# Storing the intermediate x2 once as float32, by feature block from three buffers, and splitting it in the second layer pair

## The chip, the cores and the metric

The kernel runs on one core of a Trainium2 chip. The metric is device microseconds of one execution, the median of several runs. Besides the timed runs there is one execution under the hardware profiler; all rows below are from it.

Five engines work side by side, each through its own list in order: TensorE (PE, its weight loads shown as PEld), VectorE (DVE), ScalarE (ACT), GpSimd (POOL) and SyncE (SP), which here only issues DMAs. Engines wait for each other through semaphores.

## The reference

```python
# attention with a forgetting gate, 4 x 8 heads, 768 steps, head size 48
for t in range(S):
    state = f[:, :, t, :, None] * state + einsum('bhd,bhe->bhde', k[:, :, t], v[:, :, t])
    y[:, :, t] = einsum('bhd,bhde->bhe', q[:, :, t], state)
x = y.transpose(0, 2, 1, 3).reshape(3072, 384)
# first pair of layers: 384 -> 2048 -> 384
h = x @ w_in
x2 = where(h > 0, h, exp(minimum(h, 0)) - 1) @ w_out
# second pair: 384 -> 1024 -> 384
out = ((x2 @ w1) * (x2 @ w2) @ w3) @ w_out2
```

All arrays are float32. The weights arrive as float64 bit patterns and are turned into float32 on the core.

## The kernel before

Matrix products of the two layer pairs run on operands that were split into two parts: hi, a rounded copy in the matmul format (fp32r), and lo, the float32 value minus hi. One float32 product is then three matmuls: hi by hi, hi by lo, lo by hi. The split of a tile is an ACT copy that rounds (hi) and a DVE subtract (lo).

**First pair.** The 3072 tokens are 8 tiles of 384 (index j). A tile is 16 units (index m, one unit per 128 of the 2048 hidden features); the running unit number is U. Unit U does, in this order: some attention work for the next tile; `p1_in(U)`, 9 matmuls into a PSUM bank `h` (line 584), ACT and DVE make `g` from it (587, 588, 590); `p1_split(U-1)`, which splits g (602, 603); `p1_out(U-2)`, 9 matmuls into the three PSUM banks `acc0` to `acc2`, one per block of 128 output features (616). So a tile's sums are complete two units into the next tile. Each of the three acc banks exists once, so the next tile's first matmul into a bank waits until the old sums have been read out of it.

**The end of a tile** is lines 618 to 625. For each of the three blocks i, ACT copies the bank to `oh`, DVE subtracts to get `ol`, and SP stores both to the scratch tensor `x2_scr` in HBM, which holds hi and lo of x2. The pool `o_p` has two buffers for `oh` and two for `ol`.

**Second pair.** The tokens are 6 tiles of 512, each of 8 units. `p2_load(j)` brings hi and lo of x2 for tile j from `x2_scr` in two DMAs, straight into the two matmul operands `xh` and `xl`. Unit U does `p2_in(U)`: 9 matmuls into `h`, 9 into `at` (810), an ACT copy of `h` to `a` (816), a DVE product with `at` (818) and a split of that (821, 822); and `p2_out(U-2)`: 9 matmuls into the acc banks (836). `h` has two banks. The load of tile 0 is called at unit 14 of the last first-pair tile, the load of tile j+1 in unit 2 of tile j.

**Order of the work.** Units 17 to 109 stand in the engines' lists in the order in which the code is written (`manual_schedule`). From unit 110 on, in the last two tiles of the first pair and in the whole second pair, a list scheduler of the framework sets the order on each engine. In that stretch there is much else to do: the weights of the second pair are loaded, turned into float32 by DVE (lines 81, 83, 86, 89, after an ACT step in line 74), split by ACT and POOL (509, 510), and w3 and w_out2 are multiplied together by PE in eight rows (671).

Of the kernel before, what the change touches and what calls it, by code (L numbers as in the profile page):

```python
# [9 lines left out]
F32 = mybir.dt.float32  # L10
F32R = mybir.dt.float32r
# [209 lines left out]
def main_path(ctx, tc, flag, qkf, vin, w_in, w_out, w1, w2, w3T, w_out2, ident_d, tri_d, x2_scr, out):  # L221
# [36 lines left out]
    def slot(part, k):  # L258
        return f"wb{k}" if part == "h" else "we" if k == 0 else f"wa{k - 1}"
# [346 lines left out]
    def p1_out(U):  # L606
        if not 0 <= U < NU:
            return
        j, m = divmod(U, MF)
        if m == 0:  # L610
            accs[j] = [acc_p.tile([128, 512], F32, name=f"acc{i}")[:, 0:TN] for i in range(KD)]
        ops = pairs(j, m, 1, gs.pop(U))
        for i in range(KD):
            c = slice(128 * i, 128 * i + 128)
            for n, (lw, rg) in enumerate(ops):
                nc.tensor.matmul(accs[j][i], lhsT=lw[:, 0, c], rhs=rg,  # L616
                                 start=(m == 0 and n == 0), stop=(m == MF - 1 and n == len(ops) - 1))
        if m == MF - 1:
            for i in range(KD):
                oh = o_p.tile([128, TN], F32R, name="oh")  # L620
                ol = o_p.tile([128, TN], F32R, name="ol")
                nc.scalar.activation(out=oh, in_=accs[j][i], func=AF.Copy)
                nc.vector.tensor_tensor(out=ol, in0=accs[j][i], in1=oh.bitcast(F32), op=ALU.subtract)  # L623
                for x, o in enumerate((oh, ol)):
                    nc.sync.dma_start(out=x2_scr[x, :, i, j * TN:(j + 1) * TN], in_=o.bitcast(F32))
            accs.pop(j)

    def start_late():
        att.close()
        late["u"] = ctx.enter_context(tc.tile_pool(name="u2", bufs=3))  # L630
        late["tmp"] = ctx.enter_context(ExitStack())
        late["o"] = late["tmp"].enter_context(tc.tile_pool(name="o2p", bufs=1))
        late["w3"] = late["tmp"].enter_context(tc.tile_pool(name="w3p", bufs=2))
        o2 = late["o2"] = [late["o"].tile([128, M2, DM], F32R, name=f"o2{x}") for x in "hl"]
        late["wf"] = {}
        late["row"] = 0
        late["w3t"] = {}
        late["base"] = len(jobs) + M2
        for k in range(M2):
            jobs.append((DM, [(whole(DM), wo2_u[128 * k:128 * k + 128, :])],  # L640
                         to_parts(o2[0][:, k, :], o2[1][:, k, :]), None))
        for i in range(M2):
            for k0 in (0, 4):
                src = w3T_u[128 * k0:128 * (k0 + 4), 256 * i:256 * (i + 1)].rearrange("(k p) n -> p k n", p=128)
                jobs.append((512, [(lambda f: f.rearrange("p (k n) -> p k n", k=4), src)], w3_part(i, k0), None))
        for _ in range(2):
            cv_load()
# [28 lines left out]
    xs = {}  # L676

    def p2_load(j):
        if j < NTILE2:
            xs[j] = [wp.tile([128, KD, TN2], F32R, name=slot(x, 5 + 2 * (j % 2))) for x in "hl"]  # L680
            for x, t in enumerate(xs[j]):
                nc.sync.dma_start(out=t.bitcast(F32), in_=x2_scr[x, :, :, j * TN2:(j + 1) * TN2])

    man = ExitStack()
    pro = ExitStack()
# [58 lines left out]
    for U in range(NU + LAG):  # L744
        j, m = divmod(U, MF)
        if U == MAN:
            man.enter_context(tc.manual_schedule())
        if U == MAN_B:
            man.close()
        if j == 0:  # L750
            while cv["main"] < at_job[0, m]:
                cv_step()
            quota[0] = T0_JOBS
        while lows and 2 * MF - len(lows) < 2 * (U - MF) + 4:
            low(*lows.pop(0))
        if j == 0:
            pass
        elif late:
            quota[0] = 1 + (late["row"] > rows_done)
        rows_done = late.get("row", 0)  # L760
        todo = at_slots[j > 0].get(m, []) if j < NTILE - 1 else []
        for early in (1, 0):
            for i, k in todo:
                if (k in EARLY) == early:
                    c = CPT * (j + 1) + i
                    steps[k](c)
                    if k == len(steps) - 1:
                        a_load(c + 2)
            if early and U < NU:
                p1_in(U, fill)  # L770
            if early and U >= 1:
                p1_split(U - 1)
        if j == 0 and m >= LAG:
            while cv["main"] < at_job[1, m - LAG]:
                cv_step()
        p1_out(U - LAG)
        while quota[0] > 0:
            fill()
        if j == NTILE - 2 and m == LATE_AT:
            start_late()  # L780
        if late:
            late["go"] = lambda i: U >= (NTILE - 1) * MF + 4 * (i // 4) + 3 + LAG
            w_rows()
            if j == NTILE - 1 and m % 4 == 3:
                for a in range(KD):
                    job_12(m // 4, a)
            if m == 14 and j == NTILE - 1:
                p2_load(0)
    while late["row"] < M2:
        cv_step(1)  # L790
        w_rows()
# [1 line left out]


    late["tmp"].close()
    N2 = NTILE2 * M2
    cs = {}

    def p2_in(U):
        j, m = divmod(U, M2)  # L800
        xh, xl = xs[j]
        wh, wl = w12[m // 2]
        c = slice(128 * (m % 2), 128 * (m % 2) + 128)
        ps = []
        for e in range(2):
            p = h_p.tile([128, 512], F32, name="h") if e == 0 else at_p.tile([128, 512], F32, name="at")
            n = 0
            for a in range(KD):
                for lw, rx in ((wh, xh), (wh, xl), (wl, xh)):
                    nc.tensor.matmul(p, lhsT=lw[:, a, e, c], rhs=rx[:, a, :],  # L810
                                     start=(n == 0), stop=(n == 3 * KD - 1))
                    n += 1
            ps.append(p)
            if e == 0:
                av = late["u"].tile([128, TN2], F32, name="a")
                nc.scalar.activation(out=av, in_=p, func=AF.Copy)  # L816
        cc = av
        nc.vector.tensor_tensor(out=cc, in0=ps[1], in1=av, op=ALU.mult)  # L818
        f = xt_p.tile([128, KD, TN], F32R, name="xh" if U % 2 else "xl").rearrange("p a t -> p (a t)")
        ch, cl = f[:, 0:TN2], f[:, TN2:2 * TN2]  # L820
        nc.scalar.activation(out=ch, in_=cc, func=AF.Copy)
        nc.vector.tensor_tensor(out=cl, in0=cc, in1=ch.bitcast(F32), op=ALU.subtract)
        cs[U] = (ch, cl)
# [24 lines left out]
    for U in range(N2 + LAG):  # L848
# [4 lines left out]
                cv_step()  # L853
        if U < N2:
            p2_in(U)
            if m == 2:
                p2_load(j + 1)
        while quota[0] > 0:
            fill()
        p2_out(U - LAG)  # L860
# [73 lines left out]
```

## Time and profile before

| | |
|---|---|
| runs | 884.84, 883.4, 884.22 us; median 884.22 |
| the profiled execution's own time | 883.1 us |
| its span, first to last instruction | 881.0 us |
| mean granted clock of TensorE | 0.993 of full speed |
| PE busy in the span | 845.7 us |
| DVE busy | 486.6 us |
| ACT busy | 400.1 us |
| first pair with attention | about 30 to 575 us |
| second pair | about 575 to 875 us |

The profiled execution is 1.1 us below the median and 0.3 below the lowest of the timed runs. A busy PE row counts a matmul from its start to its modelled end; since matmuls overlap, a new 128x384 one starts each 0.17 us while one alone is shown as 0.33.

### The profile page before, as it was taken

How to read it: one execution, taken by the hardware profiler on the slowest of the kernel's cores; microseconds unless marked ns; L12 is line 12 of the kernel's file. 1: busy time of each engine (PE TensorE's matmuls, PEld its weight loads, DVE VectorE, ACT ScalarE, POOL GpSimd, SP SyncE). 2: the span in 40 equal slices, each digit the busy share in tenths (PEclk: the TensorE clock that was granted, in tenths of full speed). 3: DMA queues.
4: the chain of work that ended last, by engine and by line, in shares of the span. 5: the costliest groups of instructions: out<-in, count | busy, mean ns of one | idle time of the engine just before them, and what ended most of it. 6: DMA issues, size and time to landing. Idle time of an engine off the chain costs nothing.

```text
span 881.0 us, 14419 instructions
## 1 busy us (share of the span) xinstructions
PE 845.7 (96%) x5767; PEld 741.5 (84%) x5767; DVE 486.6 (55%) x984; ACT 400.1 (45%) x785; POOL 74.9 (9%) x80
## 2 busy tenths in 40 slices
PE   7799999999999999999999899989999999999996
PEld 6465689999999999999899789968888888888885
DVE  7999687555455555464567997894222212222221
ACT  5766455455554564654655755643212212122211
POOL 3100000000000000000002323541000000000000
PEclk8999999999999999999999999999999999999999
DMA  9775131221311312213141644570202021030001
GB/s 268 217 221 168 42 96 44 62 78 43 97 43 44 96 43 53 87 43 85 55 133 41 211 145 142 192 225 21 88 20 72 36 68 41 1 107 1 36 1 39
DMA packets 43338, 77.16 MB, mean 88 GB/s; under 512 B 3376, under 2 KB 27184, under 8 KB 43264
## 3 DMA queue, kind: packets, MB, share of 16 engines
q1 hardware_dynamic: 43264, 76.17, 28.5%
q8 instruction: 47, 0.77, 0.4%
q14 instruction: 27, 0.22, 0.1%
HBM read 62.00 MB, written 14.16 MB: 86 GB/s over the span
## 4 chain that ended last, share of the span: by engine, by line
PE 77%; DVE 13%; DMA 4%; issue 3%; ACT 2%; POOL 1%; SPq 0%; DVEq 0%; POOLq 0%
PE acc L616 18%; PE h L584 17%; PE acc L836 11%; PE h L810 10%; PE at L810 10%; PE at L416 3%; PE at L355 2%; DVE wa L86 2%; DVE wa L89 2%; PE at L671 2%; DVE wa L81 2%; DMA x_scr<-ol 1%; DVE ol L623 1%; PE at L380 1%; PE at L361 1%
## 5 line engine op out<-in xcount | busy, mean ns | idle before, releaser
L616 PE MATMUL acc<-gh,wa 128*128 128x384 f32 x432 | 146.5, 370 | 0.0
L590 DVE SCALAR_TENSOR_TENSOR g<-r,h 128x384 f32<-128x384 f32 x112 | 61.7, 551 | 143.5 <-ACT r L588 143.5
L587 ACT ACTIVATE r<-h 128x384 f32<-128x384 f32 x128 | 62.4, 487 | 149.0 <-PE h L584 148.8
L818 DVE TENSOR_TENSOR a<-at,a 128x512 f32<-128x512 f32 x48 | 33.2, 691 | 172.0 <-PE at L810 170.8
L616 PE MATMUL acc<-gh,wb 128*128 128x384 f32 x336 | 116.9, 348 | 9.2 <-DVE ol L623 9.1
L584 PE MATMUL h<-xh,wa 128*128 128x384 f32 x348 | 118.3, 378 | 3.2 <-DVE gh L590 2.6
L584 PE MATMUL h<-xh,wb 128*128 128x384 f32 x336 | 113.6, 338 | 3.4 <-DVE g L590 3.4
L616 PE MATMUL acc<-gl,wb 128*128 128x384 f32 x336 | 112.5, 335 | 0.6 <-DVE gl L603 0.6
L584 PE MATMUL h<-xl,wb 128*128 128x384 f32 x336 | 112.3, 334 | 0.0
L616 PEld LDWEIGHTS acc<-gh,wa 128*128 128x128 f32 x432 | 80.7, 188 | 11.0 <-issue 0.2
L584 PEld LDWEIGHTS h<-xh,wa 128*128 128x128 f32 x348 | 65.1, 188 | 17.3 <-DVE gh L590 5.0
L816 ACT ACTIVATE a<-h 128x512 f32<-128x512 f32 x48 | 28.7, 597 | 110.7 <-PE h L810 110.7
L616 PEld LDWEIGHTS acc<-gh,wb 128*128 128x128 f32 x336 | 63.0, 188 | 13.9 <-DVE ol L623 12.1
L588 ACT ACTIVATE r<-r 128x384 f32<-128x384 f32 x128 | 67.1, 524 | 3.5
L584 PEld LDWEIGHTS h<-xh,wb 128*128 128x128 f32 x336 | 63.1, 188 | 5.1 <-DVE g L590 4.7
L616 PEld LDWEIGHTS acc<-gl,wb 128*128 128x128 f32 x336 | 63.1, 188 | 0.9 <-DVE gl L603 0.9
L584 PEld LDWEIGHTS h<-xl,wb 128*128 128x128 f32 x336 | 63.1, 188 | 0.4
L603 DVE TENSOR_TENSOR gl<-g,gh 128x384 fp32r<-128x384 f32 x112 | 62.9, 561 | 0.6 <-ACT gh L602 0.6
L602 ACT ACTIVATE gh<-g 128x384 fp32r<-128x384 f32 x112 | 57.3, 512 | 12.2 <-DVE g L590 12.1
L810 PE MATMUL h<-wb,wb 128*128 128x512 f32 x144 | 56.2, 390 | 3.1 <-ACT a L816 3.1
L810 PE MATMUL h<-wa,wb 128*128 128x512 f32 x144 | 56.0, 389 | 0.0
L810 PE MATMUL at<-wb,wb 128*128 128x512 f32 x144 | 56.0, 389 | 0.0
(145 smaller groups left out, 1537.9 us busy)
## 6 DMA issues: line engine op xcount, KB each, us to landing
qkf<-qkf_dram SPq DMA_DIRECT2D x21, 672.0 KB, 5.1
wst<-moe_w_out_dram SPq DMA_DIRECT2D x24, 384.0 KB, 3.7
wst<-moe_w_dram SPq DMA_DIRECT2D x16, 512.0 KB, 3.6
wst<-moe_w_in_dram SPq DMA_DIRECT2D x16, 384.0 KB, 4.2
wst<-moe_w_dram SPq DMA_DIRECT2D x24, 256.0 KB, 3.6
v<-vin_dram SPq DMA_DIRECT2D x23, 224.0 KB, 4.9
x_scr<-oh SPq DMA_DIRECT2D x24, 192.0 KB, 2.0
x_scr<-ol SPq DMA_DIRECT2D x24, 192.0 KB, 2.1
```

The source lines that it names most:

```text
L416: nc.tensor.matmul(yp[32 * i:32 * i + 32, a * CH:(a + 1) * CH], lhsT=w[:, i, w0:w0 + 32], rhs=x[:, i, :], start=(n == 0), stop=(n == len(o ...
L584: nc.tensor.matmul(hp, lhsT=lw, rhs=rx, start=(n == 0), stop=(n == len(ops) - 1))
L587: nc.scalar.activation(out=r, in_=hp, func=AF.Relu, scale=-1.0)
L588: nc.scalar.activation(out=r, in_=r, func=AF.Exp, scale=-1.0)
L590: nc.vector.scalar_tensor_tensor(out=g, in0=r, scalar=-1.0, op0=ALU.add, in1=hp, op1=ALU.max)
L602: nc.scalar.activation(out=gh, in_=g, func=AF.Copy)
L603: nc.vector.tensor_tensor(out=gl, in0=g, in1=gh.bitcast(F32), op=ALU.subtract)
L616: nc.tensor.matmul(accs[j][i], lhsT=lw[:, 0, c], rhs=rg, start=(m == 0 and n == 0), stop=(m == MF - 1 and n == len(ops) - 1))
L810: nc.tensor.matmul(p, lhsT=lw[:, a, e, c], rhs=rx[:, a, :], start=(n == 0), stop=(n == 3 * KD - 1))
L816: nc.scalar.activation(out=av, in_=p, func=AF.Copy)
L818: nc.vector.tensor_tensor(out=cc, in0=ps[1], in1=av, op=ALU.mult)
L836: nc.tensor.matmul(accs[j][i], lhsT=lw[:, m % 4, c], rhs=rc, start=(m == 0 and n == 0), stop=(m == M2 - 1 and n == 2))
```

## The change

The scratch tensor holds x2 once, as plain float32. At the end of a first-pair tile each of the three acc banks is copied out once: bank 0 and bank 2 by ACT, bank 1 by DVE, with no subtract. The blocks 0 and 1 go through the two buffers of `o_p`, block 2 through a buffer of its own (`gc`, from the attention pool, or from a new pool `g2` once the attention pools are closed). Three stores go out in place of six.

In the second pair a load brings three tiles of one feature block each (float32, 128x512). Tile 0 goes into the three buffers of pool `u2`, called at unit 10 of the last tile and split at unit 14; the others go into a new pool `f2` of six buffers, opened after the weight product is done, called in unit 1 of the tile before, and split one block per unit in units 3, 4 and 5. A split is, for each block, an ACT copy into `xh` (line 695 in the new file) and a DVE subtract into `xl` (696).

```diff
         if m == MF - 1:
             for i in range(KD):
-                oh = o_p.tile([128, TN], F32R, name="oh")
-                ol = o_p.tile([128, TN], F32R, name="ol")
-                nc.scalar.activation(out=oh, in_=accs[j][i], func=AF.Copy)
-                nc.vector.tensor_tensor(out=ol, in0=accs[j][i], in1=oh.bitcast(F32), op=ALU.subtract)
-                for x, o in enumerate((oh, ol)):
-                    nc.sync.dma_start(out=x2_scr[x, :, i, j * TN:(j + 1) * TN], in_=o.bitcast(F32))
+                o = late["g"].tile([128, TN], F32, name="gc") if i == 2 and late else (
+                    e_p.tile([128, TN], F32, name="gc") if i == 2 else o_p.tile([128, TN], F32, name="o"))
+                if i % 2:
+                    nc.vector.tensor_copy(out=o, in_=accs[j][i])
+                else:
+                    nc.scalar.activation(out=o, in_=accs[j][i], func=AF.Copy)
+                nc.sync.dma_start(out=x2_scr[:, i, j * TN:(j + 1) * TN], in_=o)
             accs.pop(j)
...
+        late["g"] = ctx.enter_context(tc.tile_pool(name="g2", bufs=1))
...
     def p2_load(j):
         if j < NTILE2:
-            xs[j] = [wp.tile([128, KD, TN2], F32R, name=slot(x, 5 + 2 * (j % 2))) for x in "hl"]
-            for x, t in enumerate(xs[j]):
-                nc.sync.dma_start(out=t.bitcast(F32), in_=x2_scr[x, :, :, j * TN2:(j + 1) * TN2])
+            pool, nm = (late["u"], "a") if j == 0 else (late["f"], "f")
+            xs[j] = [pool.tile([128, TN2], F32, name=nm) for a in range(KD)]
+            for a, f in enumerate(xs[j]):
+                nc.sync.dma_start(out=f, in_=x2_scr[:, a, j * TN2:(j + 1) * TN2])
+
+    def p2_split(j, blocks=range(KD)):
+        if j < NTILE2:
+            if 0 in blocks:
+                xp[j] = [wp.tile([128, KD, TN2], F32R, name=slot(x, 5 + 2 * (j % 2))) for x in "hl"]
+            xh, xl = xp[j]
+            for a in blocks:
+                f = xs[j][a]
+                nc.scalar.activation(out=xh[:, a], in_=f, func=AF.Copy)
+                nc.vector.tensor_tensor(out=xl[:, a], in0=f, in1=xh[:, a].bitcast(F32), op=ALU.subtract)
...
+            if m == 10 and j == NTILE - 1:
+                p2_load(0)
             if m == 14 and j == NTILE - 1:
-                p2_load(0)
+                p2_split(0)
...
     late["tmp"].close()
+    late["f"] = ctx.enter_context(tc.tile_pool(name="f2", bufs=2 * KD))
...
-            if m == 2:
+            if m == 1:
                 p2_load(j + 1)
+            if 3 <= m < 3 + KD:
+                p2_split(j + 1, (m - 3,))
```

The lists of the engines change in three places that the prediction speaks of. First ACT at the end of tile 1, in the part that stands in written order (acc_1164 to acc_1166 are the three banks of that tile; in the new program they are called acc_1155 to acc_1157). Before:

```order
L602 ACTIVATE gh<-g 128x384
L622 ACTIVATE oh<-acc_1164 128x384
L622 ACTIVATE oh<-acc_1165 128x384
L622 ACTIVATE oh<-acc_1166 128x384
L587 ACTIVATE r<-h 128x384
```

Now:

```order
L602 ACTIVATE gh<-g 128x384
L625 ACTIVATE o<-acc_1155 128x384
L625 ACTIVATE gc<-acc_1157 128x384
L587 ACTIVATE r<-h 128x384
L588 ACTIVATE r<-r 128x384
```

ACT has two copies there in place of three, into two different buffers. DVE at the same place, before:

```order
L603 TENSOR_TENSOR gl<-g,gh 128x384
L623 TENSOR_TENSOR ol<-acc_1164,oh 128x384
L623 TENSOR_TENSOR ol<-acc_1165,oh 128x384
L623 TENSOR_TENSOR ol<-acc_1166,oh 128x384
L329 SCALAR_TENSOR_TENSOR qkf<-qkf,cmax 112x128 x4
```

Now:

```order
L603 TENSOR_TENSOR gl<-g,gh 128x384
L623 COPY o<-acc_1156 128x384
L329 SCALAR_TENSOR_TENSOR qkf<-qkf,cmax 112x128 x4
L590 SCALAR_TENSOR_TENSOR g<-r,h 128x384
L603 TENSOR_TENSOR gl<-g,gh 128x384
```

Three subtracts have become one copy. The third place is the start of the second pair, where the scheduler sets the order. ACT, from the last row of the weight product on, before:

```order
L673 ACTIVATE wb_6007<-at 128x384
L622 ACTIVATE oh<-acc_5423 128x384
L622 ACTIVATE oh<-acc_5424 128x384
L74 ACTIVATE wa_5159<-wst 128x512
L509 ACTIVATE wb_5881<-wt 128x512
L816 ACTIVATE a<-h 128x512
L74 ACTIVATE wa_5159<-wst 128x512
L622 ACTIVATE oh<-acc_5425 128x384
L509 ACTIVATE wb_5881<-wa_5159 128x512
L821 ACTIVATE xl<-a 128x512
```

Now (675 is the old 673, 835 the old 816, 840 the old 821):

```order
L675 ACTIVATE wb_5953<-at 128x384
L625 ACTIVATE o<-acc_5363 128x384
L625 ACTIVATE gc<-acc_5365 128x384
L74 ACTIVATE wa_5108<-wst 128x512
L509 ACTIVATE wb_5827<-wt 128x512
L695 ACTIVATE wb_6405<-f 128x512
L835 ACTIVATE a<-h 128x512
L695 ACTIVATE wb_6405<-f 128x512
L509 ACTIVATE wb_5827<-wa_5108 128x512
L695 ACTIVATE wb_6405<-f 128x512
L840 ACTIVATE xl<-a 128x512
```

The first copy of a split of tile 1 (it waits for its load) now stands ahead of the first `a<-h` of the second pair, and the other two ahead of the first `xl<-a`. DVE there, before:

```order
L623 TENSOR_TENSOR ol<-acc_5423,oh 128x384
L623 TENSOR_TENSOR ol<-acc_5424,oh 128x384
L89 SCALAR_TENSOR_TENSOR wt<-wst,wt 128x512
L83 TENSOR_SCALAR wa_5159<-wa_5159 128x512
L81 TENSOR_SCALAR wa_5159<-wa_5159 128x512
L86 SCALAR_TENSOR_TENSOR wa_5159<-wst,wa_5159 128x512
L83 TENSOR_SCALAR wa_5159<-wa_5159 128x512
L89 SCALAR_TENSOR_TENSOR wa_5159<-wst,wa_5159 128x512
L623 TENSOR_TENSOR ol<-acc_5425,oh 128x384
L818 TENSOR_TENSOR a<-at,a 128x512
L86 SCALAR_TENSOR_TENSOR wa_5159<-wst,wa_5159 128x512
L81 TENSOR_SCALAR wa_5159<-wa_5159 128x512
```

Now (837 is the old 818, 841 the old 822):

```order
L623 COPY o<-acc_5364 128x384
L89 SCALAR_TENSOR_TENSOR wt<-wst,wt 128x512
L83 TENSOR_SCALAR wa_5108<-wa_5108 128x512
L81 TENSOR_SCALAR wa_5108<-wa_5108 128x512
L86 SCALAR_TENSOR_TENSOR wa_5108<-wst,wa_5108 128x512
L696 TENSOR_TENSOR wa_6406<-f,wb_6405 128x512
L89 SCALAR_TENSOR_TENSOR wa_5108<-wst,wa_5108 128x512
L83 TENSOR_SCALAR wa_5108<-wa_5108 128x512
L696 TENSOR_TENSOR wa_6406<-f,wb_6405 128x512
L837 TENSOR_TENSOR a<-at,a 128x512
L86 SCALAR_TENSOR_TENSOR wa_5108<-wst,wa_5108 128x512
L696 TENSOR_TENSOR wa_6406<-f,wb_6405 128x512
```

Two 384-wide subtracts fewer stand ahead of the first `a<-at,a`, and two 512-wide ones of the split more; the third comes right behind. Later splits (tiles 2 to 5) stand at the end of the tile two before theirs, once the operand's old contents have been read.

## Rows read from the trace of the kernel before

**Rows 1.** The page: busy time, share of the span and instructions of PE.

```profile
PE 845.7 (96%) x5767; PEld 741.5 (84%) x5767; DVE 486.6 (55%) x984; ACT 400.1 (45%) x785; POOL 74.9 (9%) x80
```

**Rows 2.** What PE waited for: total us, times, longest us.

```profile
PE acc L616 <- DVE ol L623: 9.1, 8, 1.8
...
PE h L584 <- DVE g L590: 3.4, 4, 1.1
PE h L810 <- ACT a L816: 3.1, 1, 3.1
...
PE acc L836 <- DVE xl L822: 1.1, 1, 1.1
```

**Rows 3.** What ACT and DVE waited for, the two rows with x_scr.

```profile
ACT oh L622 <- DMA x_scr<-oh: 10.0, 6, 2.1
DVE ol L623 <- DMA x_scr<-ol: 9.9, 6, 2.2
```

**Rows 4.** Timeline, PE, end of tile 1: start, us, instruction, idle before.

```profile
175.92 0.34 PE L616 MATMUL acc<-gh,wa 128*128 128x384 f32 x1
177.33 0.44 PE L616 MATMUL acc<-gh,wb 128*128 128x384 f32 x1 [1.07 <-DVE ol L623]
177.60 0.34 PE L616 MATMUL acc<-gl,wb 128*128 128x384 f32 x1
```

**Rows 5.** Timeline, ACT, the same place.

```profile
173.50 0.86 ACT L622 ACTIVATE oh<-acc 128x384 fp32r<-128x384 f32 x2
175.95 0.49 ACT L622 ACTIVATE oh<-acc 128x384 fp32r<-128x384 f32 x1 [1.59 <-DMA x_scr<-oh]
```

**Rows 6.** Timeline, DVE, the same place.

```profile
176.71 0.56 DVE L623 TENSOR_TENSOR ol<-acc,oh 128x384 fp32r<-128x384 f32 x1 [1.54 <-DMA x_scr<-ol]
```

**Rows 7.** Timeline, PE, three other stalls of the first pair.

```profile
116.82 0.44 PE L616 MATMUL acc<-gl,wb 128*128 128x384 f32 x1 [0.58 <-DVE gl L603]
...
492.51 0.44 PE L616 MATMUL acc<-gh,wb 128*128 128x384 f32 x1 [1.11 <-DVE ol L623]
...
497.98 0.44 PE L616 MATMUL acc<-gh,wb 128*128 128x384 f32 x1 [1.29 <-DVE ol L623]
```

**Rows 8.** Stretches: window, length, busy PE, PEld, DVE, ACT, POOL, clock, DMA.

```profile
478.00:516.00 38.00, 32.09 (x176) 29.85 (x175) 38.00 (x66) 25.46 (x53) 14.04 (x12) 1.00 0.53 163
545.00:575.00 30.00, 30.00 (x175) 30.00 (x174) 25.24 (x44) 18.16 (x33) 16.81 (x10) 1.00 0.57 190
575.00:597.00 22.00, 17.87 (x79) 14.18 (x78) 21.35 (x30) 9.95 (x19) 9.46 (x8) 1.00 0.71 225
597.00:868.00 271.00, 271.00 (x1197) 224.36 (x1196) 68.77 (x102) 62.53 (x104) 2.18 (x2) 1.00 0.11 38
```

**Rows 9.** Timeline, ACT, start of the second pair.

```profile
585.68 0.63 ACT L509 ACTIVATE wb<-wt 128x512 fp32r<-128x512 f32 x1 [1.75 <-DVE wt L89]
586.22 0.58 ACT L816 ACTIVATE a<-h 128x512 f32<-128x512 f32 x1
```

**Rows 10.** Timeline, DVE, start of the second pair.

```profile
584.97 0.68 DVE L89 SCALAR_TENSOR_TENSOR wt<-wst,wt 128x512 uint32<-128x512 uint32 x1
...
591.81 0.68 DVE L822 TENSOR_TENSOR xl<-a,xl 128x512 fp32r<-128x512 f32 x1
```

**Rows 11.** Timeline, POOL and DVE at 560 us.

```profile
560.42 1.80 POOL L510 TENSOR_TENSOR we<-wa,wb 128x512 fp32r<-128x512 f32 x1 [3.58 <-ACT wb L509]
...
561.11 1.67 DVE L89 SCALAR_TENSOR_TENSOR wa<-wst,wa 128x512 uint32<-128x512 uint32 x1
```

**Rows 12.** Timeline, SP before the second pair.

```profile
552.36 29.07 SPq L457 DMA_DIRECT2D wst<-moe_w_dram  x18
```

**Rows 13.** DMA issues: count, KB each, us to landing.

```profile
wst<-moe_w_dram SPq DMA_DIRECT2D x24, 256.0 KB, 3.6
```

**Rows 14.** Timeline, DVE and then PE, in the second pair.

```profile
637.53 0.68 DVE L822 TENSOR_TENSOR xh<-a,xh 128x512 fp32r<-128x512 f32 x1
...
647.54 0.61 PE L836 MATMUL acc<-xh,wb 128*128 128x512 f32 x2
```

More of the change, by code (lines that the diff above doesn't have):

```diff
@@ L679, in p2_load @@
         if j < NTILE2:
-            xs[j] = [wp.tile([128, KD, TN2], F32R, name=slot(x, 5 + 2 * (j % 2))) for x in "hl"]
-            for x, t in enumerate(xs[j]):
-                nc.sync.dma_start(out=t.bitcast(F32), in_=x2_scr[x, :, :, j * TN2:(j + 1) * TN2])
+            pool, nm = (late["u"], "a") if j == 0 else (late["f"], "f")
[11 more added lines that the diff above has]
+                nc.vector.tensor_tensor(out=xl[:, a], in0=f, in1=xh[:, a].bitcast(F32), op=ALU.subtract)
+    xp = {}
     man = ExitStack()
@@ L800, in p2_in @@
         j, m = divmod(U, M2)
-        xh, xl = xs[j]
+        xh, xl = xp[j]
         wh, wl = w12[m // 2]
@@ L927 @@
     args.append(nc.dram_tensor("out_dram", (DM, NT), F32, kind="ExternalOutput").ap())
-    args.append(nc.dram_tensor("x2_scr", (2, 128, KD, NT), F32, kind="Internal").ap())
+    args.append(nc.dram_tensor("x2_scr", (128, KD, NT), F32, kind="Internal").ap())
     args.append(nc.dram_tensor("x_scr", (B, S, DM), F32, kind="Internal").ap())
```

## The prediction

> **What bounds the kernel now.** I read the page's busy times first: PE is busy 845.7 of 881.0 us [rows 1], so at most 35.3 us can be won by removing waits, and only waits of PE count. The list of what PE waited for then says which: the largest is 9.1 us in eight waits for the subtract `ol` of line 623, the end of a first-pair tile [rows 2]. The list for all engines says what that subtract waited for in turn: ACT 10.0 us and DVE 9.9 us, six times each, for the stores to x_scr [rows 3]. Six tile ends, six times the same stall, and the timeline at one of them shows its parts. ACT copies two banks at once at 173.50 and then sits 1.59 us until the first store has landed, because the third `oh` needs a buffer back [rows 5]. DVE does the same with `ol`, 1.54 us, and subtracts at 176.71 [rows 6]. PE has sent the matmul before at 175.92, wants bank 2 next, and starts it at 177.33 [rows 4].
>
> The table by stretches tells where PE waits at all. In 478 to 516 us DVE is busy all of 38.00 us and PE 32.09; in 575 to 597, where the second pair starts, DVE 21.35 of 22.00 and PE 17.87; from 597 to 868 PE is busy all the time [rows 8]. So the six tile ends have the buffer stall, these two stretches are bound by DVE's list and the rest of the second pair by PE alone; the change is costed in each by itself.
>
> **The tile ends in written order (tiles 0 to 5).** Removed per tile: three ACT copies, three DVE subtracts, six stores. Added: two ACT copies, one DVE copy, three stores, and a third buffer. No copy now needs a buffer that this tile has just used; its last use is a whole tile back, some 60 us (116.82 and 177.33 are two neighbouring tile ends [rows 4, 7]) against a wait of 1.6 [rows 5]. ACT's two copies took 0.86 us from 173.50 [rows 5], so banks 0 and 2 are out by about 174.4. PE wants bank 2 at 175.92 + 0.17 = 176.1 (matmuls follow each other at 0.17): 1.7 us spare. DVE's copy, taken at the price of the subtract, 0.56 [rows 6], ends near 174.7, in time as well.
>
> One stall's worth: 177.33 - 175.92 - 0.17 = 1.24 us, of which the row shows 1.07 because it counts from the modelled end of the matmul before; and the matmul after follows 0.27 later and not 0.17 [rows 4]. So a shown wait costs 0.26 more than shown. Six waits: 9.1 less the two at 492.51 and 497.98, 1.11 and 1.29 [rows 2, 7], is 6.7, and 6 x 0.26 makes it 8.3. After tile 0 a second stall follows, 0.58 for a `gl` that DVE had queued behind the late subtract [rows 7]; it goes too, 0.8. Sum: **-9.1 us**. What is late next is the next `g` (ACT, then DVE behind the scans), which I find about a microsecond ahead of PE. Ends: -4.5, if half of each stall is taken over by that; -9.1.
>
> **The end of tile 6 (478 to 516).** Here DVE never rests [rows 8], so taking a wait away only moves PE to the next `g` in DVE's list. What counts is DVE's work: two instructions of about 0.47 us pitch fewer, 0.9 us; the order of the weight work between the `g`s hardly changes. I take **-0.6**. Ends: +0.5, if the new order meets one more long DVE instruction, and -2.9, if both shown stalls go whole (1.11 + 1.29 + 2 x 0.26).
>
> **The split of tile 0 (unit 14).** Three ACT and three DVE instructions, 0.5 to 0.6 us each, fall in 545 to 575, where PE is busy 30.00 of 30.00, ACT 18.16 and DVE 25.24 [rows 8]. The 4.8 us that DVE has free there take the 1.8 us; up to 0.4 of it may be left over and be late at 575, and stands in the next range. If the cover were gone it would cost 1.8.
>
> **The start of the second pair (575 to 597).** PE's two stalls there are 3.1 us for `a` and 1.1 for `xl` [rows 2]. The first ends with DVE's line 89 at 584.97, ACT's line 509 at 585.68, `a` at 586.22 [rows 9, 10]. Now: DVE has one 0.47 us instruction less ahead of line 89, so 509 ends near 585.7; then ACT's first split copy waits for its load `f`, and `a<-h`, for which PE's third unit needs the bank, is queued behind it. The load is issued on SP behind two weight loads fewer than the 18 that leave by 581.43, and such a load of 256 KB lands in 3.6 us [rows 12, 13]: by 585.0 at the latest, 0.7 us before ACT gets there. So the copy costs its 0.55 us, `a` starts at about 586.3, +0.1. For the second stall, DVE has two 512-wide subtracts more and two 384-wide fewer ahead of `a<-at,a`, and one more behind: 3 x 0.60 - 2 x 0.47 = 0.9 us; in exchange a weight step of line 81 moves from ahead of `xl` to behind it. `xl`, which started at 591.81 [rows 10], is then some 0.5 later, and that has the 0.1 in it: **+0.5**. Ends: -1.0, if the order happens to be better, and +3.9, the leftover and the next paragraph added.
>
> A price on DVE that the trace shows: while POOL's subtract of 560.42 ran, 1.80 us, DVE's line 89 of 561.11 took 1.67 us and not the 0.68 of the like one at 584.97 [rows 10, 11], 1.0 more. The new subtract reads both operands from SBUF, the old one read a PSUM bank. If each of the three new ones here met POOL and added its 1.0, that would be +3.0. I count none, since a POOL instruction delays DVE once, whichever instruction it meets, and POOL's number is unchanged. The Trainium skill, page "SBUF — State Buffer", section "Who interferes with whom", speaks against the change here: a VectorE instruction with two SBUF inputs contends with a GpSimd instruction that reads SBUF, the one that starts first holds the shared port throughout, and one input from SBUF alone does not contend. The trace agrees as far as that slow row goes; by the rule the sum would be -6.2 rather than -9.2.
>
> **The second pair (597 to 868).** Four more splits, each three ACT and three DVE instructions, 3.4 us in all if done one after the other. They stand behind unit 7's `a`, so that unit's `xh` may be 3.4 us late. A subtract of 637.53 is used by PE at 647.54 [rows 14]: 9.3 us to spare. Cost 0; with the cover gone up to 4 x 3.4. The loads halve in bytes; nothing waited for them.
>
> **Sum.** -9.1 - 0.6 + 0.5 = -9.2. The profiled execution took 883.1, so 873.9; the median of the runs was 1.1 above it, which would give 875.0. I say **874.5**; each case below has the same 0.6 on top of its sum.
>
> **The rivals.**
> - *The next wait takes over.* At each tile end PE is stopped again by `g` or `gl`. For it: the `gl` stall right behind the first one [rows 7]. Against: that one was itself a child of the late subtract. -4.5 - 0.6 + 0.5: 879.1.
> - *The splits meet POOL*, as priced: +3.0, 877.5. For it: POOL is busy 9.46 of 22 us there and DVE has no slack [rows 8].
> - *More comes back.* Both stalls of tile 6 go whole and the start is not longer: -9.1 - 2.9 + 0.0, 871.7. Against: DVE's 38.00 of 38.00.
> - *It doesn't do what it says.* The buffers aren't free in time after all, because the block-2 buffer shares its place with others; the stalls stay: about 883.7.
> - *Slower.* ACT is held at the first split copy by a late load. Each microsecond after 585.7 is one on PE's path, and DVE's subtract and all of the second pair stand behind it. To be slower it must eat 9.2 + 1.8 = 11 us, that is, land after 596.7. For it: SP issues in order, and its weight loads wait for staging buffers that this same DVE list frees. Against: that queue was through at 581.43 [rows 12]. From 886.
>
> **How the numbers follow.** Forecast 0.60, its own range 872.5 to 876.5; next wait 0.14; POOL 0.10; more 0.07; nothing 0.04; slower 0.05. The range 871 to 879.5 leaves out the last two and a little of the second. Less than 0.2% (1.8 us) can't be told from no change: faster 0.91, the same 0.04, slower 0.05.
>
> **What would show it.** Right: no wait for x_scr stores left on ACT or DVE; no stall of PE in the six tile ends; DVE still busy throughout at the end of tile 6, with PE stalls for `g` of 5 to 6 us there; the stalls for `a` and `xl` about as long as before; PE without a gap in the second pair. Wrong: a PE stall of about a microsecond at the tile ends under another name (the first rival); ACT idle until a load `f` lands (the last); gaps at the tiles of the second pair.

## The result, and the profile after

The changed kernel took 876.21 us (median of four runs, 874.1 to 876.3) against 884.12 before (883.4 to 884.84, with a fourth run of 884.03): a ratio of 0.9905, 95% interval 0.9888 to 0.9922. The forecast was 874.5, with a range of 871.0 to 879.5. The profiled execution took 876.22 with a span of 874.4, so it stands 6.6 us below the span of before, where 9.2 were forecast.

First the list of what PE waited for, after (line, total us, times, longest us; it answers to [rows 2]):

```profile
PE h L829 <- ACT a L835: 5.1, 1, 5.1
...
PE h L584 <- DVE g L590: 2.9, 5, 1.1
...
PE acc L616 <- DVE gl L603: 1.6, 2, 1.1
...
PE acc L616 <- DVE o L623: 0.3, 1, 0.3
```

The 9.1 us for the end of a tile are down to 0.3. No wait of ACT or DVE for x_scr is left ([rows 3] had 10.0 and 9.9). But the wait for the first `a` of the second pair is 5.1 and was 3.1. The wait for the first `xl` (1.1) is gone from the list.

The end of tile 1, which is the place of [rows 4 to 6], on ACT, DVE and PE (start, us, instruction):

```profile
171.63 0.47 ACT L625 ACTIVATE o<-acc 128x384 f32<-128x384 f32 x1
172.00 0.48 ACT L625 ACTIVATE gc<-acc 128x384 f32<-128x384 f32 x1
```

```profile
172.28 0.55 DVE L623 COPY o<-acc 128x384 f32<-128x384 f32 x1
```

```profile
174.05 0.33 PE L616 MATMUL acc<-gh,wa 128*128 128x384 f32 x1
174.22 0.33 PE L616 MATMUL acc<-gh,wb 128*128 128x384 f32 x1
```

All three banks are out at 172.83; PE's first matmul into bank 2 starts at 174.22, at the usual distance of 0.17 from the one ahead of it.

Then the stretches of [rows 8] (columns as there; the last one is cut at 860, since the program now ends earlier). The windows are the same instants, so the work in them lies 6 to 10 us further on in the program:

```profile
478.00:516.00 38.00, 34.23 (x185) 31.47 (x184) 36.02 (x65) 24.96 (x51) 12.23 (x10) 1.00 0.57 182
545.00:575.00 30.00, 29.14 (x157) 27.34 (x155) 28.01 (x41) 15.62 (x29) 18.18 (x11) 1.00 0.39 129
575.00:597.00 22.00, 17.79 (x68) 14.55 (x69) 20.45 (x31) 11.55 (x20) 7.13 (x6) 0.84 0.57 183
597.00:860.00 263.00, 263.00 (x1162) 217.68 (x1161) 69.73 (x105) 64.33 (x108) 0.00 (x0) 1.00 0.06 22
```

PE has no gap from 597 on, as forecast. The 0.86 us that PE lacks in 545 to 575 are the start of its stall for the first `a`. The new thing is the granted clock of 0.84 in 575 to 597; before it was 1.00.

**Where the time went, instant by instant.** ACT reads every PSUM bank `h` once (line 587 in the first pair, `a<-h` in the second), so the starts of these instructions are marks that both kernels have. The table gives by how much a mark comes earlier than before, in us; from every number the lead that the execution already had at unit 17 is taken off (first column). Nothing that any of these kernels changes lies ahead of unit 17: that column is how much executions differ in what comes before (the first 108 us), from +0.5 to -1.5.

```
                              lead at   unit 101   unit 125   first a of   last a<-h
                              unit 17  (6 ends)    (540 us)    2nd pair   (the end)
the change                     +0.04      9.34       9.66        7.60        6.57
the change, again              -0.49      9.34       9.64        7.59        7.19
e1  buffers only               +0.28      9.12       9.14        9.17        9.15
e12 buffers only, again        -1.46      9.12       9.16        9.17        9.08
e2  shared third buffer        -0.23      6.47       6.82        4.91        4.46
e3  no subtracts for tile 0    +0.35      9.35       9.63        9.58        9.53
e9  these subtracts apart      -0.02      9.33       9.63        8.60        6.64
e8  these subtracts on POOL    +0.49      9.34       9.63        6.62        6.35
e5  split of tile 1 later      -1.03      9.34       9.62        8.07        7.22
e4  at twice                   -0.48      9.34       9.65        7.56        5.59
e6  half and half              +0.38      9.13       9.43       10.34        7.78
e7  half and half, reordered   -0.57      9.14       9.44       10.36        9.88
e10 start reordered            -0.04      9.12       9.43       14.37       12.33
```

So the change wins 9.34 at the six tile ends, 0.3 more at the end of tile 6, loses 2.06 between unit 125 and the first `a` of the second pair and 1.03 behind it (0.40 in the other execution). From the sixth `a` to the end the lead stays at 6.6. The experiments were made along these steps.

### The profile page after: what moved, and what is told of

Same layout as the page of the kernel before. It is cut to its first block, busy times and chain, and to the rows that moved or that the text cites. A ratio compares the mean times of both kernels' runs of the same rounds, so it can differ in the third digit from the quotient of the medians.

```text
span 874.4 us, 14388 instructions
## 1 busy us (share of the span) xinstructions
PE 848.2 (97%) x5767; PEld 744.4 (85%) x5767; DVE 490.6 (56%) x986; ACT 405.7 (46%) x795; POOL 75.1 (9%) x80
## 4 chain that ended last, share of the span: by engine, by line
PE 82%; DVE 11%; issue 2%; ACT 2%; DMA 2%; POOL 1%; SPq 0%; POOLq 0%; DVEq 0%
PE h L584 19%; PE acc L616 19%; PE acc L855 11%; PE h L829 11%; PE at L829 11%; PE at L416 4%; PE at L355 2%; DVE wa L89 2%; DVE wa L86 2%; PE at L673 2%; DVE wa L81 1%; PE at L361 1%; PE at L380 1%; DVE wa L83 1%; DMA qkf<-qkf_dram 1%
## 5 line engine op out<-in xcount | busy, mean ns | idle before, releaser
L584 PE MATMUL h<-xh,wa 128*128 128x384 f32 x348 | 120.3, 385 | 1.4 <-DVE gh L590 0.7
```

The costliest lines, as they stand in the source:

```text
L584: nc.tensor.matmul(hp, lhsT=lw, rhs=rx, start=(n == 0), stop=(n == len(ops) - 1))
```

## The experiments

**e1 and e12: the buffers alone.** The kernel before, with one thing changed: at the ends of tiles 0 to 5 the third `oh` and the third `ol` get buffers of their own.

```diff
-                oh = o_p.tile([128, TN], F32R, name="oh")
-                ol = o_p.tile([128, TN], F32R, name="ol")
+                pool, s = (e_p, "3") if i == 2 and not late else (o_p, "")
+                oh = pool.tile([128, TN], F32R, name="oh" + s)
+                ol = pool.tile([128, TN], F32R, name="ol" + s)
```

> The kernel before, with one thing changed: at the ends of tiles 0 to 5 the third oh and the third ol get buffers of their own; hi and lo are still both made and stored. If the wait for the stores is the whole price of a tile end: the third copy and subtract follow the first two at once, bank 2 is read by about 2.0 us after the first copy starts, 0.6 us before PE wants it, no stall of PE at these six ends, -8.5 to -9.3 us by 485 us, and as nothing else moved and no split is added in the second pair, all of it at the end: 874.8 to 875.8. If it is the number of instructions (one copy less on ACT, two subtracts less on DVE) that matters: most of the stall stays under the same name, 880 or more.

Measured: 874.05 us, ratio 0.9894 (0.9879 to 0.9909). DVE, the end of tile 1 in this kernel:

```profile
172.26 1.48 DVE L624 TENSOR_TENSOR ol<-acc,oh 128x384 fp32r<-128x384 f32 x3
```

Three subtracts in 1.48 us, done at 173.74, and PE takes bank 2 at 174.20 without a wait. The first theory holds: the lead at unit 101 is 9.12, and it is still 9.15 at the end. So the third buffer is enough by itself; with it, one copy and two subtracts less per tile end add the remaining 0.2. What these are worth without it is seen in e2.

The same kernel was run once more beside the change itself:

> The kernel with only the two third buffers once more, on the same chip as the change itself. First theory: 873.7 to 874.3. Rival: within 0.8 of the changed kernel.

> The changed kernel once more, on the same chip as the other three. If the buffers give 9.4 and the rest of the change takes 2.6 back: 876 to 876.5, and 2 to 2.6 more than the kernel with only the buffers. If the difference between these two is one of chips: within 0.8 of each other.

Measured: 874.78 for the buffers (873.22 to 875.29, ratio 0.9898, 0.9881 to 0.9914), 874.16 for the change (873.48 to 876.04, ratio 0.9892, 0.9875 to 0.9909). By these times the two are the same, as the rival says. In the profiles they are not: both executions of the change lose 2.05 between unit 125 and the first `a`, and end with 6.6 and 7.2; both of the buffers alone keep their 9.1. The first column spreads by 1.7 us among these four, nearly as much as the difference looked for. All eight runs of the change average 875.1, the nine of the buffers 874.2: a difference of the expected sign, and too small for these runs to be sure of. What a step does is read from the marks, not from the medians.

**e2: the third block through the two shared buffers.**

```diff
-                o = late["g"].tile([128, TN], F32, name="gc") if i == 2 and late else (
-                    e_p.tile([128, TN], F32, name="gc") if i == 2 else o_p.tile([128, TN], F32, name="o"))
+                o = o_p.tile([128, TN], F32, name="o")
```

> The changed kernel, with block 2 sent through the same two buffers as blocks 0 and 1. The third copy then waits for the first store again, to about 2.45 us after the first copy started, and takes 0.49; PE wants the bank 2.6 after: a stall of 0.3 us shown at each of the tile ends instead of 1.07, since no DVE subtract follows the copy. So of the 9.3 us won at the six ends about 2.5 to 3.5 come back: 878 to 879. If the third buffer alone were the cause of the gain, all would come back: 885. If the fewer instructions alone were, nothing would: 876.2.

Measured: 877.63, ratio 0.9932 (0.9918 to 0.9945). ACT and PE at the end of tile 1:

```profile
174.51 0.49 ACT L624 ACTIVATE o<-acc 128x384 f32<-128x384 f32 x1 [1.99 <-DMA x_scr<-o]
```

```profile
174.47 0.34 PE L616 MATMUL acc<-gh,wa 128*128 128x384 f32 x1
175.06 0.44 PE L616 MATMUL acc<-gh,wb 128*128 128x384 f32 x1 [0.24 <-ACT o L624]
```

As expected: the wait for the store is back on ACT, and PE feels only its last 0.24. The table has 2.87 less at unit 101. Each of the tile ends 1 to 5 shows a stall of 0.24 to 0.28 and takes about 0.54 off the lead (by the marks at units 33 to 101), some 0.3 more than shown, as [rows 4] had it.

But 6.47 of the 9.34 stay without the third buffer. Before, PE waited until DVE's subtract was done at 177.27, 0.83 after ACT's copy of the same bank at 176.44 [rows 5, 6]; here no subtract follows the copy, and the stall is 0.24 in place of 1.07, shorter by the same 0.83. So each of the two remedies removes most of the stall by itself, and what they win can't be added up.

**e3: no subtracts for tile 0.** The three DVE subtracts of the split of tile 0 are left out, and `xl` of that tile is filled by DMA with x2 itself, so the lo part of tile 0 is left out of the computation:

```diff
-                nc.vector.tensor_tensor(out=xl[:, a], in0=f, in1=xh[:, a].bitcast(F32), op=ALU.subtract)
+                if j == 0:
+                    nc.sync.dma_start(out=xl[:, a].bitcast(F32), in_=x2_scr[:, a, 0:TN2])
+                else:
+                    nc.vector.tensor_tensor(out=xl[:, a], in0=f, in1=xh[:, a].bitcast(F32), op=ALU.subtract)
```

> The changed kernel without the three DVE subtracts of the split of tile 0: xl of that tile is filled by three more DMAs from the scratch tensor (this leaves out that part of the computation). If these subtracts delay DVE's list of weight steps, which then runs without rest up to the first a<-h: that a starts 1.5 to 2.0 us earlier, the stall of PE for it falls from 5.1 to 3.1 to 3.6 us, and 1.5 to 2.0 us come back: 874.2 to 874.7. If the weight loads or POOL set the time of that a: within 0.3 us of 876.2.

Measured: 872.98, ratio 0.9886 (0.9871 to 0.9901); the first `a` 2.0 earlier than in the change, as the first theory says, and the end 3.0 earlier (2.3 against the other execution of the change). What PE waits for at the start of the second pair here:

```profile
PE h L832 <- ACT a L838: 3.1, 1, 3.1
...
PE acc L858 <- DVE xl L844: 1.1, 1, 1.1
```

These are the two stalls of before [rows 2], to the tenth. From unit 125 to the end this execution loses 0.10, where the two of the change lose 3.09 and 2.45: all but 0.1 of the loss goes with these three subtracts. The traces show how. In the kernel before, DVE rests behind the product row's subtract while POOL works, and the next weight step waits for ACT:

```profile
554.35 0.55 DVE L674 TENSOR_TENSOR wa<-at,wb 128x384 fp32r<-128x384 f32 x1
556.32 0.80 DVE L81 TENSOR_SCALAR wa<-wa 128x512 f32<-128x512 f32 x1 [1.42 <-ACT wa L74]
```

```profile
553.99 2.84 POOL L510 TENSOR_TENSOR w3l<-wa,w3h 128x512 fp32r<-128x512 f32 x2 [4.53 <-PE at L671]
```

DVE in the changed kernel, the same unit:

```profile
542.50 0.69 DVE L696 TENSOR_TENSOR wa<-a,wb 128x512 fp32r<-128x512 f32 x1
...
543.58 1.28 DVE L696 TENSOR_TENSOR wa<-a,wb 128x512 fp32r<-128x512 f32 x2
544.78 1.52 DVE L83 TENSOR_SCALAR wt<-wt 128x512 uint32<-128x512 uint32 x1
546.33 1.67 DVE L86 SCALAR_TENSOR_TENSOR wt<-wst,wt 128x512 uint32<-128x512 uint32 x1
548.03 0.69 DVE L89 SCALAR_TENSOR_TENSOR wt<-wst,wt 128x512 uint32<-128x512 uint32 x1
548.64 0.55 DVE L676 TENSOR_TENSOR wa<-at,wb 128x384 fp32r<-128x384 f32 x1
549.11 0.42 DVE L81 TENSOR_SCALAR wa<-wa 128x512 f32<-128x512 f32 x1
```

and POOL beside it:

```profile
544.33 3.12 POOL L510 TENSOR_TENSOR w3l<-wa,w3h 128x512 fp32r<-128x512 f32 x2 [4.58 <-PE at L673]
```

The subtracts take 1.8 us, and push the weight steps of lines 83 and 86 into the 3.1 us in which POOL subtracts. There they take 1.52 and 1.67; alone they take 0.42 and 0.69. That is 1.1 and 1.0 more, 3.9 in all. The rest of 1.42 hides as much, and 0.4 come back since line 81 then takes 0.42 and not 0.80. That leaves 2.1, and the first `a` is 2.0 late. On line 83, which reads one array, the Trainium skill has a rule of its own: page "SBUF — State Buffer", section "Who interferes with whom", counts tensor_scalar among the operations that can, if their operands allow it, go into a two-port mode, in which whoever issues first holds the shared pair and the other one blocks. The trace agrees: POOL started 0.45 ahead of line 83, which took 1.52 in place of 0.42.

**e9: the same subtracts apart.** One is put behind the product row's subtract of unit 14 and two behind that of unit 15, so into DVE's rests (`rows` is the list of these subtracts):

```diff
-                p2_split(0)
+                p2_split(0, (0,))
+            if m == 15 and j == NTILE - 1:
+                p2_split(0, (1, 2))
...
+                with tc.issue_after(rows[-2]) if j == 0 else ExitStack():
+                    nc.vector.tensor_tensor(out=xl[:, a], in0=f, in1=xh[:, a].bitcast(F32), op=ALU.subtract)
```

> The changed kernel with the three DVE subtracts of tile 0's split put where DVE rested before: one behind a product row's subtract in unit 14, two behind that of unit 15, where it waits 1.2 to 1.4 us for ACT's line 74. If the three cost time because they stand together in one unit and use up more than its rest: they mostly vanish in two rests, the first a starts 1.0 to 2.0 us earlier against PE's first matmul of the second pair, 874.2 to 875.2. If each then meets POOL's w3l subtracts, which run in the same rests, and takes 1.7 in place of 0.7: no gain, 876 to 877.

Measured: 875.72, ratio 0.9913 (0.9896 to 0.993). DVE in the second rest:

```profile
555.28 0.56 DVE L676 TENSOR_TENSOR wa<-at,wb 128x384 fp32r<-128x384 f32 x1 [1.08 <-ACT wb L675]
555.75 3.12 DVE L697 TENSOR_TENSOR wa<-a,wb 128x512 fp32r<-128x512 f32 x2
```

Each theory is half right. The first `a` comes 1.0 earlier than in the change, but the two subtracts take 3.12 in the rest and not 1.28: the rest is exactly where POOL works. And the end is no earlier (6.64): PE now waits 1.5 for the first `xl`, since a subtract of tile 1 that stands ahead of it met POOL and took 1.78. So what binds is not `a` alone, it is DVE's list up to `xl`.

**e8: these subtracts on POOL.** `nc.vector.` becomes `nc.gpsimd.` for tile 0 in the same line.

> The changed kernel with the three subtracts of tile 0's split on GpSimd, not on DVE. They take about 1.3 us each there, 3.9 in all, ahead of two w3l subtracts. If it is DVE's list that these subtracts lengthen: nearly all that leaving them out gave comes back, 873.0 to 874.0. If POOL's longer list then holds the weight steps behind it (ACT's L74 waits for w3l) and DVE meets three more POOL instructions: 875.5 to 877.5.

Measured: 877.27 (874.46 to 880.09), ratio 0.9932 (0.9909 to 0.9955). The second theory holds. DVE beside the 4.9 us that the three subtracts take on POOL, and the w3l pair behind them:

```profile
542.08 1.52 DVE L83 TENSOR_SCALAR wt<-wt 128x512 uint32<-128x512 uint32 x1
543.64 1.66 DVE L86 SCALAR_TENSOR_TENSOR wt<-wst,wt 128x512 uint32<-128x512 uint32 x1
545.23 1.64 DVE L603 TENSOR_TENSOR gl<-g,gh 128x384 fp32r<-128x384 f32 x1
546.79 1.77 DVE L89 SCALAR_TENSOR_TENSOR wt<-wst,wt 128x512 uint32<-128x512 uint32 x1
```

These four DVE instructions are each 1.0 to 1.1 longer than alone, and the first `a` is 1.0 later than with the subtracts on DVE.

**e5: the split of tile 1 later.** Its copies and subtracts stay in the units whose code calls them, behind that unit's `a` and `xl` or `xh`:

```diff
-                nc.scalar.activation(out=xh[:, a], in_=f, func=AF.Copy)
-                nc.vector.tensor_tensor(out=xl[:, a], in0=f, in1=xh[:, a].bitcast(F32), op=ALU.subtract)
+                with tc.issue_after(last[0]) if j == 1 else ExitStack():
+                    nc.scalar.activation(out=xh[:, a], in_=f, func=AF.Copy)
+                with tc.issue_after(last[1]) if j == 1 else ExitStack():
+                    nc.vector.tensor_tensor(out=xl[:, a], in0=f, in1=xh[:, a].bitcast(F32), op=ALU.subtract)
```

> The changed kernel with the split of tile 1 held in the units where the code calls it: its ACT copies behind a<-h of units 3, 4, 5 and its DVE subtracts behind the subtract xl or xh of these units. The first copy no longer stands ahead of the first a<-h (0.5 us), three subtracts (2.9 us with the long one) no longer stand ahead of the first xl. If these two are what the start of the second pair pays: the stall for a falls by 0.5, the first xl comes 2 to 3 us earlier, 0.5 to 1.5 us come back: 874.7 to 875.7. If the last weight steps (DVE, ACT, POOL) hold PE there anyway: 876.2.

Measured: 876.64, ratio 0.9922 (0.9908 to 0.9935). The first `a` comes 0.47 earlier, as expected. The end comes 0.65 earlier than in one execution of the change and 0.03 earlier than in the other, so a gain at the end isn't shown, and the times show none. That the first `xl` would come 2 to 3 us earlier was wrong: the scheduler moved other weight steps into the place of the subtracts, and `xl` itself met POOL (1.65 us).

**e4: more work for PE in the stall.** The `at` matmuls of the second unit are done twice:

```diff
+            for twice in range(1 + (U == 1 and e == 1)):
...
```

> The changed kernel, with the nine at matmuls of the second unit of the second pair done twice into the same bank (the second time gives the same sums). This puts 2.1 us of work into PE's stall of 5.1 us ahead of the third unit; about 3.0 are left, as before the change, where the granted clock stayed at 1.00. If the lower clock of 579 to 584.5 us costs time (the 18 matmuls of the third unit took 6.63 us and not 4.23, of which the wait for xl hides all but 1.0): clock 1.00 there and 1.0 less, about 875.2. If the last weight block of that unit (POOL's lo part, done at 583.1) holds PE there in any case: 876.0 to 876.3 with the clock at 1.00. If the clock falls all the same: 876.2.

Measured: 877.18, ratio 0.9926 (0.9907 to 0.9944). The third line of the expectation came: the clock was 0.66 in 580 to 585 all the same, after a stall of 3.1. PE also waits 1.5 for an `xh` later on, and the end is 1.0 later than in the change. What the lower clock costs is seen better in two executions of one kernel, the one with only the buffers. First the stretches of e1, then of e12 (columns as in [rows 8]):

```profile
575.00:580.00 5.00, 2.60 (x11) 2.18 (x12) 5.00 (x10) 2.51 (x5) 1.69 (x1) 1.00 0.81 241
580.00:585.00 5.00, 3.91 (x17) 2.91 (x16) 4.93 (x8) 1.93 (x4) 1.91 (x2) 1.00 0.95 304
```

```profile
575.00:580.00 5.00, 1.98 (x7) 1.34 (x7) 5.00 (x10) 2.72 (x5) 1.38 (x2) 0.89 0.75 244
580.00:585.00 5.00, 5.00 (x18) 3.96 (x18) 5.00 (x8) 1.78 (x4) 1.65 (x2) 0.77 0.91 265
```

The one has full clock and the wait of 1.1 for `xl`; the other has the lower clock and no such wait; they end at 9.15 and 9.08. There the clock costs no more than 0.07, since PE only reaches the wait later. In the change the lower clock is longer:

```profile
579.21 0.80 PE L829 MATMUL h<-wb,wb 128*128 128x512 f32 x1 [5.07 <-ACT a L835]
579.80 0.63 PE L829 MATMUL h<-wa,wb 128*128 128x512 f32 x1
...
584.48 0.39 PE L829 MATMUL at<-wb,wb 128*128 128x512 f32 x1
...
585.84 0.62 PE L855 MATMUL acc<-xl,wb 128*128 128x512 f32 x2
```

```profile
584.19 0.68 DVE L841 TENSOR_TENSOR xl<-a,xl 128x512 fp32r<-128x512 f32 x1
```

The first `xl` is there at 584.87. The 18 matmuls of the unit took 6.63 us here, from 579.21 to 585.84. Before, at full clock, they took 4.23:

```profile
586.85 0.50 PE L810 MATMUL h<-wb,wb 128*128 128x512 f32 x1 [3.06 <-ACT a L816]
...
591.08 0.39 PE L836 MATMUL acc<-xl,wb 128*128 128x512 f32 x1
```

At full clock PE would be at line 855 at 583.44 and wait for `xl` until about 584.9, and then send the second matmul; it sends it at 586.1. By this estimate the clock takes 1.1, and that is the whole loss behind the first `a`. No execution of the change was profiled with full clock there, so this is worked out and not shown. In the other execution of the change (e11) the lower clock was shorter:

```profile
579.75 0.80 PE L829 MATMUL h<-wb,wb 128*128 128x512 f32 x1 [5.09 <-ACT a L835]
...
585.75 0.62 PE L855 MATMUL acc<-xl,wb 128*128 128x512 f32 x2
```

The 18 matmuls took 6.00 there, 0.63 less, and the loss behind the first `a` is 0.40 in place of 1.03, less by the same 0.63. Two executions of one kernel show that much to be the clock's.

**e6, e7 and e10: versions from what was found.** e6 stores tiles 0 to 3 (j below HL) as hi and lo (third buffers as in e1) and tiles 4 to 7 as float32; tiles 0 to 2 of the second pair then need no split, and the three copies of tile 7 are on ACT.

```diff
+                if j < HL:
+                    nc.scalar.activation(out=oh, in_=accs[j][i], func=AF.Copy)
+                    nc.vector.tensor_tensor(out=ol, in0=accs[j][i], in1=ob, op=ALU.subtract)
+                elif i % 2 and j < NTILE - 1:
+                    nc.vector.tensor_copy(out=ob, in_=accs[j][i])
+                else:
+                    nc.scalar.activation(out=ob, in_=accs[j][i], func=AF.Copy)
```

> Both schemes in one kernel: tiles 0 to 3 of the first pair stored as hi and lo (third buffers as in the run with only the buffers), tiles 4 to 7 as plain float32, all three copies of tile 7 on ACT. Tiles 0 to 2 of the second pair are loaded straight into their operands, only tiles 3 to 5 are split. If splits at the start of the second pair are what costs there, and DVE's work at the end of tiles 6 and 7 too: two subtracts less than the kernel before ahead of the first a (0.9 us) and less at the end of tile 6 (0.3), on top of the 9.3 of the tile ends: 872.5 to 873.5. If the start is bound by the weight loads and not by DVE: 874.0, as with the buffers alone.

Measured: 875.53, ratio 0.9914 (0.9895 to 0.9932), 2 us above the upper end of what was expected; 7.78 at the end. The first `a` is earlier, as expected (10.34). But DVE's subtract for the first `xl` came only 0.2 earlier than in the change (with the first column taken off), behind a weight step of line 86 that met POOL and took 1.65, and PE waits 1.5 for it.

e7 holds the weight steps of the third quarter behind the first `xl`, and those of the second quarter behind the first `a`:

```diff
-            while cv["split"] < len(jobs) - 3 * (3 - m // 2):
-                cv_step()
+            with tc.issue_after(last[m // 2 - 1]) if m in (2, 4) else ExitStack():
+                while cv["split"] < len(jobs) - 3 * (3 - m // 2):
+                    cv_step()
```

> The kernel with half and half, with the weight steps of the third quarter held behind the first xl (DVE) and those of the second quarter behind the first a (ACT). If the wait for xl of 1.1 us is caused by weight steps ahead of it on DVE: it goes, 871.5 to 872.5. If the weights are then late for the fifth unit: no gain or a loss of up to 1, and PE waits for an L510 or L509 there.

Measured: 873.28, ratio 0.9879 (0.9858 to 0.99); the wait for `xl` is gone, the end at 9.88; the time is 0.8 above what was expected.

e10 starts from e6 and holds ACT's weight steps of the last two quarters behind the first `a`, and DVE's behind the first `xl` (AFTER is 6 and 5, the number of jobs counted from the last):

```diff
+    def behind(i, e):
+        return tc.issue_after(last[e]) if last[e] is not None and i >= len(jobs) - AFTER[e] else ExitStack()
...
+            with behind(i, 0):
                 jobs[i][2](cvt.pop(i)[1].bitcast(F32))
...
+        with behind(i, 1):
             doubles_to_f32(nc, [cvt[x] for x in range(i, i + k)])
```

> The half and half kernel with ACT's weight steps of the third and fourth quarter (needed by the fifth unit and later) behind the first a of the second pair, and DVE's from the second block of the third quarter on behind the first xl. If the two stalls at the start (a, 2.1 to 5.1 us, and xl, 1.1 to 1.5) come from weight steps that nobody needs yet standing ahead of a and xl: both go, PE runs from the first pair into the second with less than 1 us of waits there, 869.5 to 871. If PE needs those weights at once, or the wait for their loads now holds ACT ahead of xl: the stall only changes its name, 873 to 874.

Measured: 870.69 (869.71 to 871.39), ratio 0.9855 (0.984 to 0.9871): faster than the kernel before and than the change. ACT and DVE at the start of the second pair:

```profile
571.52 0.50 ACT L639 ACTIVATE ol<-acc 128x384 f32<-128x384 f32 x1
571.89 0.62 ACT L852 ACTIVATE a<-h 128x512 f32<-128x512 f32 x1
```

```profile
575.52 0.69 DVE L858 TENSOR_TENSOR xl<-a,xl 128x512 fp32r<-128x512 f32 x1 [2.28 <-ACT xl L857]
576.13 0.42 DVE L81 TENSOR_SCALAR wt<-wt 128x512 f32<-128x512 f32 x1
```

The first `a` comes 6.8 earlier than in the change, DVE even rests ahead of `xl`, and PE's only wait in the second pair is 0.8 us for an `xh` at 598.58. The clock stays at 1.00. So the two stalls at that place came from weight steps that PE didn't need until two or more units later.

## Why the prediction was right, and where not

- **The six tile ends, -9.1.** Right: 9.34 in the marks. The working, 0.26 more than each shown stall and the `gl` behind the first, gives the size to 0.2. e1 and e2 show the cause: the buffer alone brings 9.1. Sharing it again takes 2.9 back, so the fewer instructions alone, which the text didn't weigh apart, are worth 6.5. The rival that another wait takes over at these ends didn't come.
- **The end of tile 6, -0.6.** Right in sign, 0.3 in size. As argued, both stalls of [rows 7] for `ol` go (to 0.3) and come back in part, as waits for `g` and `gl`: PE's waits of that place are 4.8 us in all, 5.8 before. The sign that was named, 5 to 6 us of stalls for `g`, is not quite met: 2.9 are for `g`, 1.6 for `gl`.
- **The split of tile 0, 0.** This term failed: 2.06 from unit 125 to the first `a`, of which 2.0 go with the three subtracts (e3), more than the 1.8 that the text gave for no cover at all. It was hidden, by the text, in the 4.8 us that DVE has free in 545 to 575. That sum is made of rests of 1.4 us and less, mostly one per unit, and the three subtracts stand in one unit. Besides, "a POOL instruction delays DVE once, whichever instruction it meets" was wrong: before the change POOL's pair there met a resting DVE. The rival on POOL was right in mechanism: at least 1.0 per meeting, and lines 83 and 86 and the first subtract of tile 1 (1.74 us) met it. Its place was wrong, though: most of it falls in unit 14 and not at the start of the second pair, and DVE's rest hides a part.
- **The start of the second pair, +0.5.** 1.03 and 0.40 behind the first `a` in two executions, inside the ends of -1.0 to +3.9, and that is luck. The part for `a` was right: the copy ahead of it costs its 0.5 (e5), the DVE instruction fewer ahead of line 89 gives as much back, and without the subtracts of tile 0 the first `a` is 0.05 late (e3), where +0.1 was forecast. The part for `xl` was not: a lower clock, which was not thought of, takes the place of the wait for it.
- **The second pair, 0.** Right: the lead doesn't change from the sixth `a` on.
- **A late load** was not seen: ACT's first split copy started at 578.06, right behind line 509.

The sum by the marks is 9.34 + 0.32 - 2.06 - 1.03 = 6.57 in place of 9.2. The forecast time was right within its range because the large term was right, and the small ones, which had come out near zero for reasons that in part were wrong, took back less than a third of it.

## What to carry to other kernels

Before a transfer is made smaller to remove a wait, give the waiting tile one more buffer and look: here that alone gave 9.1 of the 9.3 us won at the tile ends, and kept them to the end, where the change kept 6.6 to 7.2. Work added to an engine that is idle 16% of a stretch is not free if that idle time is cut into short rests, in each of which DVE waits for another engine; look at the rest in the unit where the work lands, and at what runs beside it. Where a busy engine's list decides when PE goes on, look at what stands ahead of the awaited instruction and isn't needed yet: holding it back gave 4.5 us here (12.33 in e10 against 7.78 in e6).

## What the runs showed of the hardware

The granted clock at the start of the second pair fell to its lower level (matmuls 0.43 apart and not 0.23, 1.2 GHz in place of 2.4) in some executions and not in others of the same kernel, after the same stall of 3.0 us (e1 and e12). It came behind stalls of 2.1 us (e6, e7), 3.0 (e12), 3.1 (e4) and up to 6.0 (e8), and not behind 3.0 (e1) and 3.1 (the kernel before, e3): the length of the stall alone doesn't decide it here, and what does stays open. And the part ahead of everything changed here, the first 108 us, differs by up to 2 us among executions (first column of the table), which is why kernels 1 us apart couldn't be told from each other by their medians.
